# Attention with 64x64 score tiles, paired value products and unpadded q, ahead of two feed-forward nets

## The chip, the core and the metric

The kernel runs on one core of a Trainium2 chip, alone. The core has engines that run side by side, each with its own in-order queue: TensorE (PE; its weight loads are shown apart as PEld), VectorE (DVE), ScalarE (ACT), GpSimd (POOL), and SyncE (SP), which here only issues DMA transfers. [...] The metric is the device time of one execution in microseconds (us); of the kernel before three executions are known.

## What is computed

Banded attention with block summaries, for 2 batches, 8 heads, 768 positions and 64 numbers per head, and then two feed-forward nets on the 1536 x 512 result:

```python
k_sum = k.reshape(B, H, nb, 32, D).max(axis=3)
v_sum = v.reshape(B, H, nb, 32, D).mean(axis=3)
mask_l = np.abs(pos[:, None] - pos[None, :]) < 16
scores_l = where(mask_l, q @ k.T / sqrt(D), -1e9)
scores_s = q @ k_sum.T / sqrt(D) + log(32)
a = softmax(concatenate([scores_l, scores_s], -1))
x = a @ concatenate([v, v_sum], axis=2)      # heads side by side: 1536 x 512
h = x @ w_in;   x = (h - tanh(h)) @ w_out            # first net, 512 -> 2048 -> 512
h = x @ w2_in;  out = (h * tanh(softplus(h))) @ w2_out
```

Everything is float32. The attention's products are plain float32 matmuls; those of the nets are three products of split halves (`xhi`, `xlo`, `ghi`, `glo`, and the two halves of the weights).

## The kernel before

**Attention.** The queries are cut into 12 units u of 128 rows (6 for each batch), and the 8 heads into 4 pairs; head e of a pair (e = 0 or 1) lies on partitions 64e to 64e+63 of q and k. Of a unit's 128 rows, rows 0 to 63 (s = 0) and 64 to 127 (s = 1) each see a window of 96 keys and 24 block summaries, so a score row has 120 columns. In `qk(u, e)` there are 8 matmuls (4 pairs, 2 values of s) of a 128 x 64 piece of q against 128 x 120 of k; the 64 partitions of the other head are zeros in `qz`, so that all 128 partitions can be contracted. The scores of e = 0 go to a PSUM bank of tag `s`, of e = 1 to one of tag `tr`; each tag has two banks. `softmax(u, e)` reduces on DVE and takes the exponent on ACT, `norm(u)` divides (on POOL, four times on DVE), `a_trans(u, e)` turns the weights with 4 full-array transposes into `aT` and has them copied to `asb` (by DVE where the table `ASB_DVE` says so, otherwise by ACT), and `av(u, e)` multiplies them with the values in 8 matmuls of 120 x 64 against 120 x 64, into the half of a bank `x` on partitions 64e to 64e+63. `x_hi` and `x_lo` take the result out. `v_trans` (once for each batch) turns the value summaries through a bank of `tr`.

**What sets the order.** The order is written out by hand. Step j issues, in this order: `x_hi`, `qk` of (u, e) = j, `softmax` of j-1, `norm`, `x_lo`, `a_trans` of j-5, `av` of j-6, and then the DMA loads and reductions of the table `todo`. From step 24 on there are no scores any more, and `more_in` puts first products of the first net (`ffn_in`, 12 matmuls of 512 columns, called FFN-in 0, 1, 2, ... below) between the last steps of attention: FFN-in 0 at step 24, 1 at step 25, 2 at step 29. Behind attention the nets' products follow each other on TensorE. Weights are loaded raw and converted in `conv_tick`, as pieces that go through ACT (`conv_top`, L114), DVE (`conv_or`, L121), ACT or POOL (`conv_hi`, L130, L132) and DVE or POOL (`conv_lo`, L137); FFN-in i needs both of its pieces.

**Loads.** All DMAs are issued by SP in program order. A DMA waits for the one eight before it in that order to have landed (they share a semaphore), and for its tile to be free: q of unit u for the scores of u-3, v of u for the value products of u-3. `load_q(u)` issues two DMAs, of 64 partitions each. `q_zero` writes the zeros once, on DVE and ACT, at the program's start.

Of the kernel before, what the change touches and what calls it, by code (L numbers as in the profile page):

```python
# [9 lines left out]
F32 = mybir.dt.float32  # L10
# [10 lines left out]
BLK, WIN, T = 32, 16, 64  # L21
# [5 lines left out]
def kernel(  # L27
# [17 lines left out]
    nc = tc.nc  # L45
    NU, _, HP, _ = qt_d.shape
# [4 lines left out]
    NB = S // BLK  # L51
    KA = NB + KW
# [25 lines left out]
    def pst(tag):  # L78
        return ps.tile([128, 512], F32, tag=tag, name=tag)
# [99 lines left out]
    def attention(actx):  # L179
# [3 lines left out]
        kq = kq_x.enter_context(tc.tile_pool(name="kq", bufs=1))  # L183

        NK = UPB + 2
        kt = [kq.tile([128, HP, KU + 2 * NB], F32, name=f"kt{n}") for n in range(NK)]
        qz = [kq.tile([128, 2, HP, 128], F32, name=f"qz{n}") for n in range(3)]
        vu = [con.tile([KA, 2, H, D], F32, name=f"vu{n}") for n in range(3)]
        masks = [con.tile([128, KA], F32, name=f"mask{m}") for m in range(3)]
        ident = con.tile([128, 128], F32, name="ident")  # L190
        SUM = ((0, NB), (KW, KA))
        WND = ((NB, KA), (0, KW))

        def q_zero(n):
            for e in range(2):
                other = qz[n][64 * (1 - e):64 * (1 - e) + 64, e]
                if n < 2:
                    nc.vector.memset(other, 0.0)
                else:
                    nc.scalar.copy(other, qz[0][64 * (1 - e):64 * (1 - e) + 64, e])  # L200

        def constants():
            nonlocal tops
            make_identity(nc, ident)
            k_edges(0)
            for m in range(3):
                nc.gpsimd.memset(masks[m], 0.0)
                for s in range(2):
                    rows = masks[m][T * s:T * s + T]
                    nc.gpsimd.memset(rows[:, SUM[s][0]:SUM[s][1]], math.sqrt(D) * math.log(BLK))  # L210
                    reg = rows[:, WND[s][0]:WND[s][1]]

                    conds = [([[1, KW]], -1, -1), ([[-1, KW]], 2 * WIN - 1, 1)]
                    if (m, s) == (0, 0):
                        conds.append(([[1, KW]], -WIN, 0))
                    if (m, s) == (2, 1):
                        conds.append(([[-1, KW]], KW - WIN - 1, 0))
                    for pattern, base, mul in conds:
                        nc.gpsimd.affine_select(
                            out=reg, in_=reg, pattern=pattern, base=base, channel_multiplier=mul,  # L220
                            compare_op=ALU.is_ge, fill=-BIG,
                        )
            k_edges(UPB)
            tops = top_tiles(2)
# [20 lines left out]
                nc.gpsimd.memset(kt[UPB - 1][:, :, r:r + WIN], 0.0)  # L245

        def load_q(u):
            for e in range(2):
                nc.sync.dma_start(out=qz[u % 3][64 * e:64 * e + 64, e], in_=qt_d[u, 64 * e:64 * e + 64])

        def load_v(u):
            for s in range(2):
# [2 lines left out]
        def load_vt(b, g):  # L255
            vtc[b, g] = two.tile([128, HP, 256], F32, tag="vtc", name="vtc", bufs=3)
            nc.sync.dma_start(out=vtc[b, g], in_=vt_d[b, g])
# [48 lines left out]

        sums, neg, aa, asb, xps, sc = {}, {}, {}, {}, {}, {}

        def qk(u, e):
            p = pst(("s", "tr")[e])  # L310
            pv = p[:, 0:HP * KA].rearrange("p (a n) -> p a n", a=HP)
            for hp in range(HP):
                for s in range(2):
                    k0 = s * (NB + T)
                    nc.tensor.matmul(
                        out=pv[T * s:T * s + T, hp, :],
                        lhsT=qz[u % 3][:, e, hp, T * s:T * s + T],
                        rhs=kt[u % NK][:, hp, k0:k0 + KA],
                    )
            sc[u, e] = pv  # L320

        def softmax(u, e):
            w, pv = u % UPB, sc.pop((u, e))
# [37 lines left out]
                nc.scalar.activation(out=t, in_=pv, func=ACTF.Copy)  # L361
            asb[u, e] = t

        def av(u, e):
            if e == 0:
                xps[u] = pst("x").rearrange("p (a n) -> p a n", a=HP)
            for hp in range(HP):
                for s in range(2):
                    nc.tensor.matmul(  # L369
                        out=xps[u][64 * e:64 * e + 64, hp, T * s:T * s + T],  # L370
                        lhsT=vu[u % 3][:, s, 2 * hp + e, :],
                        rhs=asb[u, e][:, hp, T * s:T * s + T],
                    )

        def x_hi(u):
            c, o = divmod(u * 128, CH)
            nc.scalar.activation(out=xhi[c][:, :, o:o + 128], in_=xps[u], func=ACTF.Copy)

        def x_lo(u):
            c, o = divmod(u * 128, CH)  # L380
            nc.vector.tensor_tensor(
                out=xlo[c][:, :, o:o + 128], in0=xps.pop(u),
                in1=xhi[c][:, :, o:o + 128].bitcast(F32), op=ALU.subtract,
            )
# [13 lines left out]
        load_vt(0, 1)  # L398
        load_q(2)
        load_vt(0, 2)  # L400
        for n in range(3):
            q_zero(n)
        constants()
        warm = pst("x")
        for n in range(NWARM):
# [34 lines left out]
        NJ = 2 * NU  # L440
        LT, LA = 5, 6

        def ticks(j, counts):
            for _ in range(counts.get(j, 0)):
                conv_tick(len(pieces) // 2, j in HI_POOL, j in LO_POOL)

        for j in range(NJ + LA + 2):
            if j in (NJ, NJ + 1, NJ + 5):
                more_in(n_in)
            if j == NJ:  # L450
                kq_x.close()
                more_w(4)
            xu, xr = divmod(j - LA - 2, 2)
            if xu >= 0 and not xr:
                x_hi(xu)
            if j < NJ:
                qk(j // 2, j % 2)
            nu, nr = divmod(j - 3, 2)
            nr = nr == 0 and 0 <= nu < NU
            if 1 <= j <= NJ:  # L460
                softmax(*divmod(j - 1, 2))
            ticks(j, AHEAD)
            if nr:
                norm(nu)
            if xu >= 0 and xr:
                x_lo(xu)
            if LT <= j < NJ + LT:
                a_trans(*divmod(j - LT, 2))
            if j in before_av:
                before_av[j]()  # L470
            if LA <= j < NJ + LA:
                av(*divmod(j - LA, 2))
            for f in todo.get(j, []):
                f()
            ticks(j, AFTER)
            if NJ + 2 <= j <= NJ + 3:
                gate_1(steps[j - NJ - 2])
            if j == NJ + 4:
                gate_1s(steps[0])
# [39 lines left out]
    def gate_1s(z):  # L519
        g_hi(z, ts[z])  # L520
        g_lo(z, ts.pop(z))
# [73 lines left out]
    def more_in(n):  # L595
        nonlocal n_in
        while n_in <= min(n, NS - 1):
            ffn_in(*steps[n_in])
            n_in += 1
# [18 lines left out]
    def more_w(n):  # L618
        wb = ctx.enter_context(tc.tile_pool(name=f"wb{len(W)}", bufs=1))
        for i in range(len(W), len(W) + n):  # L620
            W[i] = wb.tile([128, 2, 1024], F32R, name=f"w{i}")

    with tc.manual_schedule():
        with ExitStack() as actx:
            attention(actx)
# [140 lines left out]
```

## Time and profile before

| | us |
|---|---|
| median of 3 runs (lowest, highest) | 611.64 (611.49, 612.99) |
| profiled execution | 611.33 |
| its span, first to last instruction | 609.6 |
| TensorE busy (share of the span) | 594.0 (97%) |
| VectorE busy | 421.1 (69%) |
| ScalarE busy | 330.2 (54%) |
| GpSimd busy | 53.2 (9%) |

Times in the rows are us from the span's start. The profile shows each float32 matmul of the attention as two matmul records; transposes and the nets' products are one record each. Matmuls are pipelined, so a record lasts longer than the step from one record to the next. In a timeline row stand start, length, engine, line, operation, output <- inputs, shape, count, and in brackets the engine's idle time just before it and what ended it. In the chain of waits, which is followed back from the end, stand start, share of time and what it was; there a record counts only for the time it adds. [...]

### The profile page before, as it was taken

The numbers are of one execution on the slowest core, as the hardware profiler recorded it, in microseconds if no ns is written. First come the engines' busy times: TensorE is split into PE (matmuls) and PEld (weight loads), VectorE is DVE, ScalarE is ACT, GpSimd is POOL, SyncE is SP. The second block draws the span as 40 slices with busy tenths as digits, with TensorE's granted clock in tenths as the row PEclk, the third lists the DMA queues.
The fourth block names the chain that finished last, engine by engine and source line by source line (L and its number), as shares of the span: only waits on it lengthen the run. The fifth ranks groups of instructions, "written<-read, shape, count | busy, mean of one in ns | idle before, by whom it ended". The sixth has DMA issues, their size and how long they took to land.

```text
span 609.6 us, 9228 instructions
## 1 busy us (share of the span) xinstructions
PE 594.0 (97%) x3212; PEld 494.0 (81%) x3212; DVE 421.1 (69%) x972; ACT 330.2 (54%) x793; POOL 53.2 (9%) x109
## 2 busy tenths in 40 slices
PE   7698999999999999999999999999999999999997
PEld 6577888888888888888888888888888888888886
DVE  6668967887342222367777579997768777598785
ACT  5678958887242222356776446664454444454442
POOL 5446652000000000000000000000000000000000
PEclk9899999999999999999999999999999999999999
DMA  9999547766121000125662101100010000100001
GB/s 239 232 254 261 162 134 230 230 216 198 45 54 33 1 0 1 34 83 160 198 195 74 52 1 52 53 19 1 1 69 1 1 1 0 70 1 1 1 1 69
DMA packets 32302, 52.20 MB, mean 86 GB/s; under 512 B 3392, under 2 KB 25920, under 8 KB 32256
## 3 DMA queue, kind: packets, MB, share of 16 engines
q1 hardware_dynamic: 32256, 51.62, 29.3%
q8 instruction: 25, 0.41, 0.3%
q14 instruction: 21, 0.17, 0.1%
HBM read 48.07 MB, written 3.15 MB: 84 GB/s over the span
## 4 chain that ended last, share of the span: by engine, by line
PE 90%; DMA 7%; SPq 1%; DVE 1%; POOL 0%; ACT 0%; issue 0%; POOLq 0%
PE s L486 7%; PE aT L486 7%; PE s L487 7%; PE aT L487 7%; PE s L488 7%; PE tr L487 7%; PE x L487 7%; PE aT L488 7%; PE tr L488 7%; PE x L488 7%; PE tr L486 7%; PE x L486 7%; DMA qz<-in_qt_dram 3%; DMA kt<-in_kw_dram 2%; PE x L369 2%; PE aT L355 1%
## 5 line engine op out<-in xcount | busy, mean ns | idle before, releaser
L511 DVE TENSOR_TENSOR glo<-t,ghi 128x512 fp32r<-128x512 f32 x48 | 33.4, 696 | 86.9 <-ACT ghi L506 86.9
L506 ACT ACTIVATE ghi<-t 128x512 fp32r<-128x512 f32 x48 | 30.2, 629 | 97.3 <-PE tr L488 97.3
L486 PE MATMUL s<-xhi,w 128*128 128x512 f32 x192 | 74.9, 390 | 0.0
L486 PE MATMUL aT<-xhi,w 128*128 128x512 f32 x192 | 74.9, 390 | 0.0
L487 PE MATMUL s<-xlo,w 128*128 128x512 f32 x192 | 74.7, 389 | 0.0
L488 PE MATMUL s<-xhi,w 128*128 128x512 f32 x192 | 74.7, 389 | 0.0
L487 PE MATMUL aT<-xlo,w 128*128 128x512 f32 x192 | 74.7, 389 | 0.0
L488 PE MATMUL aT<-xhi,w 128*128 128x512 f32 x192 | 74.7, 389 | 0.0
L114 ACT ACTIVATE top<-raw 128x256 f16<-128x256 bf16 x128 | 61.5, 486 | 12.3 <-ACT w L132 5.3
L121 DVE SCALAR_TENSOR_TENSOR cv<-raw,top 128x256 int32<-128x256 int32 x128 | 55.5, 435 | 11.3 <-ACT top L114 7.7
L132 ACT ACTIVATE w<-cv 128x256 fp32r<-128x256 f32 x120 | 47.6, 402 | 10.7 <-DVE cv L121 9.7
L137 DVE TENSOR_TENSOR w<-cv,w 128x256 fp32r<-128x256 f32 x114 | 48.4, 426 | 0.1
L542 DVE SCALAR_TENSOR_TENSOR t<-n,r 128x512 f32<-128x512 f32 x48 | 33.1, 689 | 17.5 <-ACT r L539 17.3
L335 ACT ACTIVATE aa<-aa,neg 128x120 f32<-128x120 f32 x96 | 36.6, 383 | 15.0 <-DVE neg L330 15.0
L511 DVE TENSOR_TENSOR glo<-n,ghi 128x512 fp32r<-128x512 f32 x48 | 33.1, 690 | 15.3 <-ACT ghi L506 15.3
L506 ACT ACTIVATE ghi<-n 128x512 fp32r<-128x512 f32 x48 | 30.3, 631 | 24.3 <-PE tr L487 16.1
L486 PEld LDWEIGHTS s<-xhi,w 128*128 128x128 f32 x192 | 36.0, 188 | 7.6
L486 PEld LDWEIGHTS aT<-xhi,w 128*128 128x128 f32 x192 | 36.0, 188 | 7.6
L488 PEld LDWEIGHTS s<-xhi,w 128*128 128x128 f32 x192 | 36.1, 188 | 7.5
L488 PEld LDWEIGHTS aT<-xhi,w 128*128 128x128 f32 x192 | 36.1, 188 | 7.5
L487 PEld LDWEIGHTS s<-xlo,w 128*128 128x128 f32 x192 | 36.0, 188 | 7.4
L487 PEld LDWEIGHTS aT<-xlo,w 128*128 128x128 f32 x192 | 36.0, 188 | 7.4
(99 smaller groups left out, 1307.6 us busy)
## 6 DMA issues: line engine op xcount, KB each, us to landing
raw<-in_w_dram SPq DMA_DIRECT2D x128, 255.8 KB, 3.6
vu<-in_vw_dram SPq DMA_DIRECT2D x24, 192.0 KB, 6.0
qz<-in_qt_dram SPq DMA_DIRECT2D x24, 128.0 KB, 6.9
vtc<-in_vt_dram SPq DMA_DIRECT2D x6, 512.0 KB, 6.8
out_dram<-o SPq DMA_DIRECT2D x9, 256.0 KB, 2.1
kt<-in_kw_dram SPq DMA_DIRECT2D x6, 320.0 KB, 6.4
kt<-in_kw_dram SPq DMA_DIRECT2D x6, 256.0 KB, 4.3
out_dram<-t SPq DMA_DIRECT2D x3, 256.0 KB, 2.1
```

Of the source, the lines that this page charges most:

```text
L114: nc.scalar.activation(out=tops[n % len(tops)].bitcast(F16).rearrange("p (n t) -> p n t", t=2)[:, :, 1], in_=raws[n].bitcast(BF16).rearran ...
L121: nc.vector.scalar_tensor_tensor(out=tmps[n], in0=raws.pop(n).bitcast(I32).rearrange("p (n t) -> p n t", t=2)[:, :, 0], scalar=13, in1=top ...
L132: nc.scalar.activation(out=hi, in_=t, func=ACTF.Copy)
L137: (nc.gpsimd if on_pool else nc.vector).tensor_tensor(out=W[i][:, 1, o:o + PW], in0=tmps.pop(n).bitcast(F32), in1=W[i][:, 0, o:o + PW].bit ...
L335: nc.scalar.activation(out=aa[u][:, e, hp, :], in_=aa[u][:, e, hp, :], func=ACTF.Exp, scale=-1.0, bias=neg[u][:, e, hp:hp + 1], accum_out= ...
L369: nc.tensor.matmul(out=xps[u][64 * e:64 * e + 64, hp, T * s:T * s + T], lhsT=vu[u % 3][:, s, 2 * hp + e, :], rhs=asb[u, e][:, hp, T * s:T ...
L486: nc.tensor.matmul(out=out, lhsT=w[0], rhs=x[0], start=first, stop=False)
L487: nc.tensor.matmul(out=out, lhsT=w[0], rhs=x[1], start=False, stop=False)
L488: nc.tensor.matmul(out=out, lhsT=w[1], rhs=x[0], start=False, stop=last)
L506: nc.scalar.activation(out=ghi, in_=t, func=ACTF.Copy)
L511: nc.vector.tensor_tensor(out=glo, in0=t, in1=ghi.bitcast(F32), op=ALU.subtract)
L542: nc.vector.scalar_tensor_tensor(out=ts[z], in0=ns[z], scalar=2.0, in1=rs[z], op0=ALU.add, op1=ALU.mult)
```

## The change

`qk(u)` now issues both heads of a pair in turn, without zeros: a matmul contracts 64 partitions, and four of them (2 values of e, 2 of s) use the four 64 x 64 quarters of the array. `av(u)` issues the two heads in turn, so that consecutive matmuls write different halves of the PSUM partitions. `qk(u)` stands at step 2u, and `av(u)` at step 2u+7, where before the halves stood at 2u, 2u+1 and 2u+6, 2u+7. The zeros go, and q comes in one DMA of 128 partitions. The number of matmuls stays.

```diff
-        def q_zero(n):
-            for e in range(2):
-                other = qz[n][64 * (1 - e):64 * (1 - e) + 64, e]
...
         def load_q(u):
-            for e in range(2):
-                nc.sync.dma_start(out=qz[u % 3][64 * e:64 * e + 64, e], in_=qt_d[u, 64 * e:64 * e + 64])
+            nc.sync.dma_start(out=qt[u % 3], in_=qt_d[u])
...
-        def qk(u, e):
-            p = pst(("s", "tr")[e])
-            pv = p[:, 0:HP * KA].rearrange("p (a n) -> p a n", a=HP)
+        def qk(u):
+            for e in range(2):
+                sc[u, e] = pst(("s", "tr")[e])[:, 0:HP * KA].rearrange("p (a n) -> p a n", a=HP)
             for hp in range(HP):
                 for s in range(2):
-                    k0 = s * (NB + T)
-                    nc.tensor.matmul(
-                        out=pv[T * s:T * s + T, hp, :],
-                        lhsT=qz[u % 3][:, e, hp, T * s:T * s + T],
-                        rhs=kt[u % NK][:, hp, k0:k0 + KA],
-                    )
+                    for e in range(2):
+                        d = slice(64 * e, 64 * e + 64)
+                        k0 = s * (NB + T)
+                        nc.tensor.matmul(
+                            out=sc[u, e][T * s:T * s + T, hp, :],
+                            lhsT=qt[u % 3][d, hp, T * s:T * s + T],
+                            rhs=kt[u % NK][d, hp, k0:k0 + KA],
+                        )
...
-        def av(u, e):
-            if e == 0:
-                xps[u] = pst("x").rearrange("p (a n) -> p a n", a=HP)
+        def av(u):
+            xps[u] = pst("x").rearrange("p (a n) -> p a n", a=HP)
             for hp in range(HP):
                 for s in range(2):
...
+                    for e in range(2):
+                        nc.tensor.matmul(
+                            out=xps[u][64 * e:64 * e + 64, hp, T * s:T * s + T],
...
-            if j < NJ:
-                qk(j // 2, j % 2)
+            if j < NJ and j % 2 == 0:
+                qk(j // 2)
...
-            if LA <= j < NJ + LA:
-                av(*divmod(j - LA, 2))
+            if LA <= j < NJ + LA and (j - LA) % 2:
+                av((j - LA) // 2)
```

TensorE's queue around unit 9 before, from the value products of the end of unit 5 (x) over the scores of unit 9 (s, tr) to the products of unit 6; aT are transposes, and a row counts matmuls of the program:

```order
L369 MATMUL x<-asb,vu_102 64x64 x8
L315 MATMUL s<-kt_90,qz_97 64x120 x8
L355 MATMUL aT<-ident,aa 120x128 x4
L369 MATMUL x<-asb,vu_100 64x64 x8
L315 MATMUL tr<-kt_90,qz_97 64x120 x8
L355 MATMUL aT<-ident,aa 120x128 x4
L369 MATMUL x<-asb,vu_100 64x64 x8
```

The same place with the change:

```order
L285 MATMUL tr<-ident,vsum 24x128 x4
L363 MATMUL x<-asb,vu_102 64x64 x16
L310 MATMUL s<-kt_90,qt_97 64x120
L310 MATMUL tr<-kt_90,qt_97 64x120
...
L349 MATMUL aT<-ident,aa 120x128 x8
L363 MATMUL x<-asb,vu_100 64x64 x16
```

The second half of the scores moved up in front of the transposes, alternating with the first (16 single rows); two sets of transposes now stand together, and both halves of the value products behind them.

SP's queue in step 5 before, from the loads of q for units 4 and 5 to the loads of k for units 9 and 10 (kt_90, kt_91); L303 copies value summaries within SBUF, and DMAHWn is the semaphore that every eighth DMA shares:

```order
L249 DMA qz_98<-in_qt_dram 64x512 [waits DMAHW2_49,PE_49]
L229 DMA kt_89<-in_kw_dram 128x4x160 [waits DVE_49,DMAHW3_49,Activation_49,Pool_49]
L249 DMA qz_99<-in_qt_dram 64x512 [waits DMAHW4_49,PE_49]
L249 DMA qz_99<-in_qt_dram 64x512 [waits DMAHW5_49,PE_49]
L303 DMA vu_101<-vu_100 24x512 [waits DMAHW6_49,Activation_49]
L303 DMA vu_101<-vu_100 24x512 [waits DMAHW7_49,Activation_49]
L303 DMA vu_102<-vu_100 24x512 [waits DMAHW0_49]
L303 DMA vu_102<-vu_100 24x512 [waits DMAHW1_49]
L229 DMA kt_90<-in_kw_dram 128x4x160 [waits DMAHW2_49,DVE_49]
L229 DMA kt_91<-in_kw_dram 128x4x160 [waits DMAHW3_49,DVE_49]
```

And with the change:

```order
L221 DMA kt_96<-in_kw_dram 128x4x160 [waits DMAHW3_49]
L240 DMA qt_98<-in_qt_dram 128x512 [waits DMAHW5_49,PE_49]
L221 DMA kt_89<-in_kw_dram 128x4x160 [waits DVE_49,DMAHW6_49,Activation_49,Pool_49]
L240 DMA qt_99<-in_qt_dram 128x512 [waits DMAHW7_49,PE_49]
L294 DMA vu_101<-vu_100 24x512 [waits DMAHW0_49,Activation_49]
L294 DMA vu_101<-vu_100 24x512 [waits DMAHW1_49,Activation_49]
L294 DMA vu_102<-vu_100 24x512 [waits DMAHW2_49]
L294 DMA vu_102<-vu_100 24x512 [waits DMAHW3_49]
L221 DMA kt_90<-in_kw_dram 128x4x160 [waits DMAHW4_49,DVE_49]
L221 DMA kt_91<-in_kw_dram 128x4x160 [waits DMAHW5_49,DVE_49]
```

Each unit has one DMA less, so "eight before" reaches further back: kt_90 waited for the second half of q of unit 4, and now waits for k of unit 7, which stands before it.

## Rows read from the trace of the kernel before

**Rows 1.** Busy us by stretch (instructions in brackets), PEclk, DMA share, GB/s

```profile
core 0: us, PE busy (x) PEld busy (x) DVE busy (x) ACT busy (x) POOL busy (x), PEclk, DMA share, GB/s
...
10.35:22.42 12.07, 8.70 (x105) 7.28 (x105) 9.59 (x57) 8.43 (x41) 7.14 (x17) 0.86 1.06 262
...
39.20:58.43 19.23, 16.79 (x239) 14.35 (x237) 18.67 (x91) 15.46 (x66) 12.57 (x22) 1.00 1.04 253
58.43:73.46 15.03, 15.03 (x216) 12.99 (x217) 13.36 (x64) 13.23 (x58) 7.66 (x13) 1.00 0.59 167
73.46:91.42 17.96, 17.96 (x155) 14.79 (x153) 11.79 (x29) 11.80 (x33) 10.35 (x14) 1.00 0.50 144
91.42:605.80 514.38, 514.37 (x2270) 425.59 (x2268) 351.72 (x672) 265.48 (x540) 4.42 (x7) 1.00 0.20 62
```

**Rows 2.** TensorE's waits from 58.6 us on: total, times, longest

```profile
PE s L315 <- DMA qz<-in_qt_dram: 0.5, 1, 0.5
```

**Rows 3.** The chain that ended last: start, us, what

```profile
50.90 7.48 DMA qz<-in_qt_dram
...
68.51 0.88 PE s L315 x15
69.39 0.58 PE aT L355 x4
69.97 1.02 PE x L369 x15
```

**Rows 4.** The DMA engines at 28 us, and SP's issues then

```profile
28.00:30.00 2.00, 1.33 (x26) 1.33 (x28) 1.97 (x11) 2.00 (x11) 1.04 (x2) 1.00 0.50 118
...
28.42 1.51 SPq L229 DMA_DIRECT2D kt<-in_kw_dram  x2
```

**Rows 5.** DVE's timeline: start, us, operation, idle before and what ended it

```profile
4.04 1.51 DVE L264 TENSOR_REDUCE ksum<-kt 128x16 f32<-128x512 f32 x2 [0.73 <-DMA kt<-in_kw_dram]
...
60.09 0.69 DVE L359 COPY asb<-aT 120x512 f32<-120x512 f32 x1 [1.43 <-PE aT L355]
...
70.36 0.68 DVE L359 COPY asb<-aT 120x512 f32<-120x512 f32 x1
...
78.25 1.04 DVE L347 TENSOR_TENSOR aa<-aa,rd 128x480 f32<-128x480 f32 x1
...
81.45 0.69 DVE L359 COPY asb<-aT 120x512 f32<-120x512 f32 x1 [1.57 <-PE aT L355]
```

**Rows 6.** TensorE's timeline, same columns

```profile
17.07 1.22 PE L315 MATMUL s<-kt,qz 128*64 128x120 f32 x15 [2.53 <-DMA qz<-in_qt_dram]
...
68.18 0.32 PE L315 MATMUL s<-kt,qz 128*64 128x120 f32 x1
...
68.35 0.22 PE L369 MATMUL x<-asb,vu 120*64 120x64 f32 x1
...
73.46 0.50 PE L486 MATMUL s<-xhi,w 128*128 128x512 f32 x1
...
85.74 0.65 PE L355 MATMUL aT<-ident,aa 128*120 128x128 f32 x4
...
91.42 0.50 PE L486 MATMUL aT<-xhi,w 128*128 128x512 f32 x1
...
94.27 0.39 PE L486 MATMUL s<-xhi,w 128*128 128x512 f32 x1
```

**Rows 7.** ACT's and POOL's timelines, same columns

```profile
57.39 1.18 ACT L296 ACTIVATE vu<-tr 24x512 f32<-24x512 f32 x2
...
86.49 0.60 ACT L361 ACTIVATE asb<-aT 120x512 f32<-120x512 f32 x1
...
74.75 0.75 POOL L137 TENSOR_TENSOR w<-cv,w 128x256 fp32r<-128x256 f32 x1
...
79.51 0.98 POOL L347 TENSOR_TENSOR aa<-aa,rd 128x480 f32<-128x480 f32 x1
...
91.58 2.56 POOL L137 TENSOR_TENSOR w<-cv,w 128x256 fp32r<-128x256 f32 x3 [1.42 <-ACT w L132]
```

More of the change, by code (lines that the diff above doesn't have):

```diff
@@ L186, in attention @@
         kt = [kq.tile([128, HP, KU + 2 * NB], F32, name=f"kt{n}") for n in range(NK)]
-        qz = [kq.tile([128, 2, HP, 128], F32, name=f"qz{n}") for n in range(3)]
+        qt = [kq.tile([128, HP, 128], F32, name=f"qt{n}") for n in range(3)]
         vu = [con.tile([KA, 2, H, D], F32, name=f"vu{n}") for n in range(3)]
@@ L192, in attention @@
         WND = ((NB, KA), (0, KW))
-        def q_zero(n):
-            for e in range(2):
-                other = qz[n][64 * (1 - e):64 * (1 - e) + 64, e]
[L197 to L200, printed above, removed]
         def constants():
@@ L307, in attention @@
         sums, neg, aa, asb, xps, sc = {}, {}, {}, {}, {}, {}
-        def qk(u, e):
-            p = pst(("s", "tr")[e])
-            pv = p[:, 0:HP * KA].rearrange("p (a n) -> p a n", a=HP)
+        def qk(u):
+            for e in range(2):
+                sc[u, e] = pst(("s", "tr")[e])[:, 0:HP * KA].rearrange("p (a n) -> p a n", a=HP)
             for hp in range(HP):
                 for s in range(2):
-                    k0 = s * (NB + T)
-                    nc.tensor.matmul(
-                        out=pv[T * s:T * s + T, hp, :],
-                        lhsT=qz[u % 3][:, e, hp, T * s:T * s + T],
-                        rhs=kt[u % NK][:, hp, k0:k0 + KA],
-                    )
-            sc[u, e] = pv
+                    for e in range(2):
[6 more added lines that the diff above has]
+                        )
         def softmax(u, e):
@@ L362, in a_trans @@
             asb[u, e] = t
-        def av(u, e):
-            if e == 0:
-                xps[u] = pst("x").rearrange("p (a n) -> p a n", a=HP)
+        def av(u):
+            xps[u] = pst("x").rearrange("p (a n) -> p a n", a=HP)
             for hp in range(HP):
                 for s in range(2):
[L369 to L373, printed above, removed]
+                    for e in range(2):
+                        nc.tensor.matmul(
+                            out=xps[u][64 * e:64 * e + 64, hp, T * s:T * s + T],
+                            lhsT=vu[u % 3][:, s, 2 * hp + e, :],
+                            rhs=asb[u, e][:, hp, T * s:T * s + T],
+                        )
         def x_hi(u):
@@ L400, in attention @@
         load_vt(0, 2)
-        for n in range(3):
-            q_zero(n)
         constants()
```

## The prediction

> **What bounds the kernel now.** I read the table by stretch first, then TensorE's waits, then the chain, then the timelines of the engines that the chain names. The table [rows 1] shows four stages. Up to 58.43 us the DMA engines are full (share 1.04 in 39.20 to 58.43), and so, in that stretch, is DVE (18.67 of 19.23 us). From 58.43 on TensorE has no idle time until its last matmul at 605.80: its only wait there is 0.5 us for q of unit 9, at 58.43 itself [rows 2]. That q is the last link of the DMA stage: 7.48 us in the queue from 50.90 on [rows 3]. So what the change saves before 58.43 is worth only what it makes that q (and DVE's work beside it) come earlier, and what it saves behind 91.42 is nothing, since there it touches nothing: 514.37 us of net products stay. The time is set by when the nets' products run without a break. The gain must come from 58.43 to 91.42, 33.0 us in which attention's last units share TensorE with FFN-in 0, 1 and 2.
>
> **What one product costs.** In the chain, 15 or 16 score records take 0.88 us, four transposes 0.58 and 15 value records 1.02 [rows 3]. The scores of one half already use two column tiles (s = 0 and 1) at once, the value products of one half only one. That column tiles do run side by side is in the trace: the first score record starts at 68.18, while value records on other columns go on until one that starts at 68.35 [rows 6]. So a value pair of 32 records should take what 16 take now, 1.05 us for 2.1. For the scores the two heads now lie on different rows of the array, and no row of the trace shows two row tiles at once: 32 records take between 0.88 us (four at once) and 1.76 (two at once). I take 0.88, since the same engine overlaps column tiles without loss, and keep 1.76 as a rival. [...]
>
> Per unit TensorE saves 0.9 + 1.05, or about 2 us. In 58.43 to 91.42 stand the scores of units 9, 10, 11 and the value products of 6 to 11: 3 x 0.9 + 6 x 1.05 = 9 us less work in 33. That would be the gain if TensorE alone set the time. It will not, because DVE is nearly as full in the first half: 13.36 of 15.03 us, and 1.43 of the rest is one wait, before 60.09 [rows 1, 5].
>
> **58.43 to 73.46.** DVE stands idle for 1.43 us until 60.09, for transposes queued behind the scores of unit 9 [rows 5]. Those scores took 1.04 us for one half; both halves now take 0.9. Their second bank is the one that `v_trans` used, which ACT empties at 58.57 (57.39 + 1.18) [rows 7], 0.14 behind the start at 58.43. So DVE's work starts at 60.1 as before, and it runs through the same list at the same pace. TensorE, now early, waits for it: the value products of unit 8 need DVE's copy of 70.36 [rows 5], which ends at 71.04. Before, they were done at 73.46; now 71.04 + 1.05 = 72.1. FFN-in 0, whose weights are long ready, starts 1.4 us earlier. A wait for DVE takes the place of most of TensorE's saving (5.9 us saved to here, 1.4 gained); queued behind the waiting value products is FFN-in 0 and nothing that DVE needs soon.
>
> **73.46 to 94.27.** An FFN-in takes 2.85 us (91.42 to 94.27) [rows 6]. From 72.1: FFN-in 0 and transposes to 75.5. FFN-in 1 needs the weight piece that POOL ends at 75.50 (74.75 + 0.75) [rows 7], so it just runs: to 78.4, transposes to 79.0, value pair of unit 9 to 80.05, transposes to 80.6. The next transposes need POOL's product that ends at 80.49 [rows 7]: to 81.2. The value pair of unit 10 needs two copies by DVE. The first stood at 81.45 and had waited 1.57 us for TensorE; DVE is done with its normalisation at 79.29 (78.25 + 1.04) [rows 5] and has one 0.7 us subtraction in between, so the copies end by 81.5. The pair runs to 82.6, and the last transposes to 83.2, which before started at 85.74 and ended at 86.4 [rows 6]: 3.2 us earlier. FFN-in 2 to 86.05, last value pair to 87.1, where it was 91.42: 4.3 us earlier.
>
> But FFN-in 4 had no slack. Its weight pieces left POOL at 94.14 (91.58 + 2.56) [rows 7], and it started at 94.27 [rows 6]. These pieces go through ACT behind its last copy, which stood at 86.49 [rows 7] and waited for those last transposes. They move by 3.2 us, to 90.9, while TensorE would be there at 87.1 + 2.85 = 89.95. It waits about 1 us, and from there everything is 3.3 us earlier. **This term: -3.3 us**; bounds -2.4 (a part of the conversions that does not move with ACT) and -4.3 (all of it does).
>
> **The DMA stage.** At 28 to 30 us the DMA share falls to 0.50 [rows 4], the one gap of the stage: 1.0 us lost. SP was held in the copies of value summaries and issued the next k at 28.42. With one DMA less per unit the "eight before" of that k is an earlier transfer, so it goes out sooner. If the gap closes, every later landing, and DVE's full stretch that begins at 39.20, moves up. Bounds: 0, if SP is held elsewhere, and -1.0. **I take -0.5.** I see no loss here: the bytes and their order are the same.
>
> **At nothing.** The removed zeros stand on DVE and ACT in the first 3.3 us; DVE's next work still waits for k at 4.04 [rows 5], so that wait covers them. Twelve issues on SP fewer: SP is ahead of the DMA engines. The value products of the first half, now one step later, have no reader before the second half is done.
>
> Changing modes is a price. At 68.18 the scores slip in among value records since both use 64-column tiles of all rows [rows 6]; with 64 x 64 tiles they may not, which costs that 0.17 us, and the first record in a new shape takes 0.50 for 0.39 (73.46 against 94.27) [rows 6]. [...] By the rows the price is at most 0.3 us per unit, and TensorE waits for DVE where it falls; at the value pairs behind 73.46 the modes are those of before. [...]
>
> **Sum.** 0.5 + 3.3 = 3.8 us. The profiled execution took 611.33 (span 609.6 and 1.7 around it), 0.3 less than the median of 611.64. It would take 607.5; against the median that is 607.8.
>
> **Rivals.** (1) The row halves run one after the other: the scores of unit 9 take 1.76, DVE starts 0.7 later, and with it all that follows: 608.5. For it: no row of the trace shows row tiles.
>
> (2) TensorE's clock falls once near 58 us. [...] With the change TensorE has about half the work in the DMA stage: 16.79 less some four units at 2 us, in 19.23 us. If a low stretch meets the scores of unit 9, these and the transposes take 2.9 for 1.5 us, and DVE starts 1.4 later: 609.2. Against it: in 39.20 to 58.43 TensorE idled 2.4 us in all and PEclk stayed 1.00 [rows 1].
>
> (3) Nothing runs side by side as meant (tiles collide, or issue is too slow): the work is as before, DVE waits 0.7 us more at 60.09, FFN-in follows as it did, and the DMA term stays: 611.1 to 612, no change.
>
> [...]
>
> **How the numbers follow.** Forecast 0.52 (606 to 609, by the bounds of its two terms), rival 1 0.11, rival 2 0.16 (608.7 to 610.5), rival 3 0.12, rival 4 0.09. Time: 607.8. The range goes from 605.8, both terms at their best and half a us more, to 610.8, which takes in rival 2 and a little of rival 3 and leaves out about 0.2. A difference under 0.3% (1.8 us: 609.8 and 613.5) can hardly be told from none. Faster: 0.52 + 0.11 + half of rival 2 = 0.71; same: the other half and most of rival 3 = 0.19; slower 0.10.
>
> **What would show it.** Right: a value pair in about 1.05 us and 32 score records in 0.9; DVE's copy at 60.1 or up to 1 us earlier, and its list until 76 unchanged; TensorE idle before the value products of unit 8, for DVE's copy, and before FFN-in 4, for POOL; FFN-in 0 near 72 and FFN-in 4 near 90.5. The prediction is wrong if q of unit 9 lands later than 58.4, if PEclk drops below 1.00 behind 55 us, if score records of the two heads never start closer than those of one, or if TensorE waits again behind 95 us.

## The result, and the profile after

The changed kernel took 602.73 us (median of 4, 602.28 to 604.61) where the kernel before took 612.32 beside it (4 runs, 611.49 to 613.78): a ratio of 0.9846, 95% interval 0.982 to 0.9872. The forecast was 607.8 with a range of 605.8 to 610.8, so the direction was right and the gain of 9.6 us was two and a half times the forecast 3.8; the time lies below the range. The profiled execution took 603.07 us, with a span of 601.3 where before had 609.6. Each kernel below was run beside the kernel before, but not all of them on the same chip, so across kernels the ratio compares better than the time. Executions more than 1.5% above the quickest of their kernel are left out of the ratios, not of the medians.

First the table by stretch of the changed kernel, which answers [rows 1] (busy us by engine, then PEclk, the granted TensorE clock with 1.00 as full speed, DMA share, GB/s). Its stretches are cut at its own events: k of unit 11 landed, scores of unit 9 (all but two records that started at 53.05), FFN-in 0, FFN-in 3, last matmul.

```profile
core 0: us, PE busy (x) PEld busy (x) DVE busy (x) ACT busy (x) POOL busy (x), PEclk, DMA share, GB/s
34.58:54.65 20.07, 13.72 (x253) 11.17 (x253) 18.33 (x92) 16.03 (x67) 12.73 (x22) 0.91 0.96 274
54.65:68.29 13.64, 11.82 (x215) 9.95 (x215) 11.94 (x59) 11.60 (x51) 6.96 (x12) 0.87 0.51 149
68.29:83.09 14.80, 14.64 (x155) 11.91 (x152) 11.48 (x31) 12.69 (x38) 11.04 (x15) 1.00 0.55 163
83.09:597.50 514.41, 514.38 (x2272) 425.74 (x2268) 352.86 (x675) 265.70 (x541) 4.42 (x8) 1.00 0.20 63
```

The last stretch is what it was (514.41 us for 514.37), so all of the gain lies ahead of FFN-in 3, as the prediction said. The timelines then show in which part. DVE's, which answers [rows 5] (the copy behind the scores of unit 9 stood at 60.09, that of unit 8's weights at 70.36):

```profile
34.58 0.69 DVE L255 TENSOR_REDUCE ksum<-kt 128x16 f32<-128x512 f32 x1 [1.31 <-DMA kt<-in_kw_dram]
...
56.31 0.69 DVE L353 COPY asb<-aT 120x512 f32<-120x512 f32 x1 [1.63 <-PE aT L349]
...
66.47 0.68 DVE L353 COPY asb<-aT 120x512 f32<-120x512 f32 x1
```

And TensorE's, which answers [rows 6] (four scores of unit 9, value products of units 7 and 8, FFN-in 0, the last value pair, FFN-in 3 and 4):

```profile
54.65 0.31 PE L310 MATMUL tr<-kt,qt 64*64 64x120 f32 x1 [1.18 <-ACT vu L287]
54.65 0.31 PE L310 MATMUL s<-kt,qt 64*64 64x120 f32 x1
54.66 0.31 PE L310 MATMUL tr<-kt,qt 64*64 64x120 f32 x1
54.67 0.31 PE L310 MATMUL s<-kt,qt 64*64 64x120 f32 x1
...
62.11 1.15 PE L363 MATMUL x<-asb,vu 120*64 120x64 f32 x30 [1.65 <-DVE asb L353]
...
66.80 1.56 PE L363 MATMUL x<-asb,vu 120*64 120x64 f32 x32
68.29 0.50 PE L478 MATMUL s<-xhi,w 128*128 128x512 f32 x1
...
82.01 1.15 PE L363 MATMUL x<-asb,vu 120*64 120x64 f32 x32
83.09 0.50 PE L478 MATMUL aT<-xhi,w 128*128 128x512 f32 x1
...
85.95 0.39 PE L478 MATMUL s<-xhi,w 128*128 128x512 f32 x1
```

Below, **the mark** is DVE's copy at 60.09 before and 56.31 after: it is the same instruction of the program in all kernels, the first that follows the scores of unit 9. The span then falls into four parts:

| part | before | after | difference | forecast |
|---|---|---|---|---|
| start to the mark | 60.09 | 56.31 | -3.8 | -0.5 |
| the mark to FFN-in 0 | 13.37 | 11.98 | -1.4 | -1.4 |
| FFN-in 0 to FFN-in 3 | 17.96 | 14.80 | -3.2 | -3.0 |
| FFN-in 3 to the end | 518.2 | 518.2 | 0 | +1.0 |

Two terms miss: the DMA stage by 3.3 us, and the wait at FFN-in 4 by 1.0.

Where the DMA stage gained is seen in the list of DMA issues (number, KB each, median us from issue to landing). Of the kernel before:

```profile
vu<-in_vw_dram SPq DMA_DIRECT2D x24, 192.0 KB, 6.0
qz<-in_qt_dram SPq DMA_DIRECT2D x24, 128.0 KB, 6.9
```

Of the changed kernel:

```profile
vu<-in_vw_dram SPq DMA_DIRECT2D x24, 192.0 KB, 4.9
qt<-in_qt_dram SPq DMA_DIRECT2D x12, 256.0 KB, 4.9
```

The loads of v were not touched, and they land in 4.9 us instead of 6.0. A q of 256 KB lands sooner than a half of 128 KB did. The bytes flow faster while the DMA share says "full" in both: from 40 to 50 us the kernel before moved 259 GB/s at a share of 1.04 (its row stands below), and the changed kernel

```profile
40.00:50.00 10.00, 7.38 (x138) 6.39 (x138) 8.67 (x45) 9.38 (x42) 7.97 (x17) 0.83 1.06 321
```

### The profile page after: what moved, and what is told of

It reads as the page before. It is cut to its first block, busy times and chain, and to the rows that moved or that the text cites. A ratio compares the mean times of both kernels' runs of the same rounds, so it can differ in the third digit from the quotient of the medians.

```text
span 601.3 us, 9203 instructions
## 1 busy us (share of the span) xinstructions
PE 578.8 (96%) x3212; PEld 479.0 (80%) x3212; DVE 417.8 (69%) x968; ACT 328.5 (55%) x791; POOL 53.4 (9%) x109
## 4 chain that ended last, share of the span: by engine, by line
PE 88%; DMA 4%; DVE 3%; ACT 2%; SPq 1%; issue 1%; POOL 0%; ACTq 0%
PE aT L478 7%; PE aT L479 7%; PE tr L479 7%; PE x L479 7%; PE aT L480 7%; PE tr L480 7%; PE x L480 7%; PE x L478 7%; PE tr L478 7%; PE s L479 7%; PE s L478 7%; PE s L480 7%; DMA kt<-in_kw_dram 3%; ACT aa L329 1%; DMA vtc<-in_vt_dram 1%; PE x L363 1%
```

## The experiments

**The two halves of the change apart.** My theory after the result was A: the loads of q, in one DMA of 128 partitions, shorten the DMA stage. The rival B: the shorter TensorE work releases tiles sooner, and the loads follow. Two kernels undo one half each, and two more split the loads and the value products.

Undo the loads alone:

```diff
-            nc.sync.dma_start(out=qt[u % 3], in_=qt_d[u])
+            for e in range(2):
+                nc.sync.dma_start(out=qt[u % 3][64 * e:64 * e + 64], in_=qt_d[u, 64 * e:64 * e + 64])
```

> The changed kernel with q loaded as before, in two DMAs of 64 partitions for each unit; all else stays. The changed kernel took 602.7 us (0.9846 of the kernel before), 5.8 us less than my sum for it had from the DMA stage and the tail at their middle; by its trace DVE's copy behind the scores of unit 9 stood 3.8 us earlier, where I had 0.5. Theory A (the loads of q: one DMA of 128 partitions makes the DMA stage shorter): those 3.8 us go, 606.5 us, and that copy stands near 60. Rival B (the order on TensorE: half as long scores and products release tiles sooner, and the loads follow): 602.7, the copy near 56.3.

Measured: 609.67 us, 0.9976 of before (0.995 to 1.0002), with the mark at 61.45. Nearly all of the gain is gone: theory A, and more than the 3.8 us it had asked for. The tail kept its part (11.98 us from the mark to FFN-in 0, 14.82 from there to FFN-in 3).

Keep the loads, undo the order on TensorE (the scores still contract 64 partitions, without zeros):

```diff
-        def qk(u):
+        def qk(u, e):
...
-            if j < NJ and j % 2 == 0:
-                qk(j // 2)
+            if j < NJ:
+                qk(j // 2, j % 2)
...
-            if LA <= j < NJ + LA and (j - LA) % 2:
-                av((j - LA) // 2)
+            if LA <= j < NJ + LA:
+                av(*divmod(j - LA, 2))
```

> The order of the kernel before on TensorE (one half of the scores and of the value products in each step), with q without zeros in one DMA; so at most two tiles can run side by side. Theory A (loads of q): it keeps the 3.8 us of the DMA stage and nothing of the tail: 608.5 us, 0.994 of the kernel before. Rival B (order): as the kernel before, 612.

Measured: 612.41 us (608.11 to 618.30, ten runs), 1.0007 (0.9969 to 1.0045), with the mark at 59.68. Theory A fails here as it stood: taken together, the runs show no gain from the quick loads alone. Why is in the table by stretch. The kernel before:

```profile
30.00:40.00 10.00, 9.37 (x136) 7.99 (x133) 5.28 (x31) 7.18 (x31) 2.82 (x3) 1.00 1.03 262
40.00:50.00 10.00, 9.28 (x136) 7.99 (x134) 9.85 (x50) 7.47 (x33) 7.36 (x13) 1.00 1.04 259
```

The old order with the quick loads:

```profile
30.00:40.00 10.00, 10.00 (x135) 8.69 (x133) 7.72 (x44) 8.01 (x34) 2.20 (x3) 0.92 0.70 209
40.00:50.00 10.00, 10.00 (x140) 8.41 (x138) 8.43 (x45) 8.52 (x35) 7.45 (x14) 1.00 0.82 259
```

The DMA share falls to 0.70 and 0.82: the loads are no longer the limit. But TensorE (first number) is busy for 10.00 of 10.00 us. Its timeline in that run repeats without a gap:

```profile
41.83 1.04 PE L306 MATMUL s<-kt,qt 64*64 64x120 f32 x16
42.80 0.65 PE L345 MATMUL aT<-ident,aa 128*120 128x128 f32 x4
43.38 1.15 PE L359 MATMUL x<-asb,vu 120*64 120x64 f32 x16
44.46 1.04 PE L306 MATMUL tr<-kt,qt 64*64 64x120 f32 x16
```

A step of half a unit takes 44.46 - 41.83 = 2.63 us, 5.25 for a unit. In the kernel before, the scores of units 5 to 9 followed each other by 5.7 to 6.3 us, at a DMA share of 1.02 to 1.06. So TensorE's limit lay close below that of the loads, and the change lowers both.

By these paces this kernel should gain some 0.4 to 1.1 us for each unit. Against that stands the clock: from the first scores of unit 3 to those of unit 4 TensorE was never idle and its granted clock was 0.50, and half a unit took 4.73 us where it later took 2.63, which is 4.2 us for the two halves. Their rows, the old order with the quick loads:

```profile
21.58:26.31 4.73, 4.73 (x36) 3.97 (x37) 2.23 (x13) 1.82 (x8) 0.81 (x1) 0.50 1.04 299
26.31:31.04 4.73, 4.73 (x37) 3.97 (x36) 2.74 (x17) 2.30 (x11) 1.93 (x2) 0.50 0.60 159
```

The kernel before had a clock of 1.00 in that part (22.42 to 29.43 us). The three quickest of the ten runs, at 608.1 to 608.4 us, came out at theory A's 608.5; their mean clock was 0.988 to 0.990, that of the others 0.974 to 0.986. Lowering one limit alone thus gained almost nothing as measured (0.9976 and 1.0007), and both together give 0.9846; how much the quick loads alone would gain at full clock, no run shows.

**What of the loads.** q in two DMAs of 128 partitions:

```diff
-            nc.sync.dma_start(out=qt[u % 3], in_=qt_d[u])
+            for e in range(2):
+                nc.sync.dma_start(out=qt[u % 3][:, 2 * e:2 * e + 2], in_=qt_d[u][:, 2 * e:2 * e + 2])
```

> The changed kernel with q in two DMAs of 128 partitions, each with two of the four pairs of heads: as many DMAs as before the change, but no half of the partitions left out. Theory A1 (transfers of 64 partitions are slow and hold the others up): 602.7, as the changed kernel. Theory A2 (the number of DMAs: one more for each unit, so that eight before in the order reaches less far back and SP is held longer): 606.5. Rival B (TensorE's order): 602.7.

Measured: 604.93 us, 0.99 (0.9866 to 0.9934), the mark at 58.58. It lies clear of the halves (0.995 to 1.0002): with as many DMAs, most of the gain is there. Then two DMAs of 64 partitions, but of every second one:

```diff
-            nc.sync.dma_start(out=qt[u % 3], in_=qt_d[u])
+            for e in range(2):
+                nc.sync.dma_start(out=qt[u % 3][e:128:2], in_=qt_d[u, e:128:2])
```

> The changed kernel with q in two DMAs of 64 partitions, as in the run with halves (0.9976), but of every second partition, where that one took the lower 64 and then the upper 64; packets of 2048 bytes and 24 DMAs in both. [...] Theory N (64 partitions as such, fewer packets in each DMA, are slow): 0.9976 and near 142 ns.

Measured: 603.5 us, 0.988 (0.9847 to 0.9912), the mark at 56.35. Same number of DMAs, same bytes and rows as the halves, and the loss is gone. So it is not the 64 partitions, it is which 64. The packets of 2048 bytes took 124 ns on average ahead of 58 us, with halves 142; those of 4096 bytes, which belong to loads that neither kernel touches, 191 and 231. With halves TensorE's clock was lower too (0.50 from 20 to 30 us, here 0.73), and what that adds to the loss is not separated by these two. DVE's row at the mark, with halves and then with every second partition:

```profile
61.45 0.69 DVE L354 COPY asb<-aT 120x512 f32<-120x512 f32 x1 [1.79 <-PE aT L350]
```

```profile
56.35 0.69 DVE L354 COPY asb<-aT 120x512 f32<-120x512 f32 x1 [2.16 <-PE aT L350]
```

**The price of the way by itself.** A kernel without attention and nets only loaded q, in four ways:

```diff
+        for rep in range(3):
+            for load in (whole, halves, every_second, pairs):
+                for u in range(8):
+                    load(u)
```

> No attention and no nets: only q of 8 units is loaded, 12 times over, each time in one of four ways: whole (128 partitions in one DMA), lower and upper 64 partitions, every second partition, two pairs of heads each; then one column of each tile is read, and the next 8 units follow. The output is zeros. It measures the price of the way by itself. If the half of the partitions is what is slow, the 2 MB in halves take longer and their packets of 2048 bytes are slower than those of every second partition, by about the 15 to 20% that the stage showed (142 against 120 ns). If the ways are alike here, halves cost only where other loads run beside them.

It could not decide: SP mostly needed 0.54 to 0.59 us to issue each DMA of 64 partitions, so only some 205 GB/s were asked for and the DMA engines were not full (with halves 207 GB/s at a share of 0.6 to 0.7 from 45.8 to 48.7 us; with every second partition 211 at 0.71 from 17.00 to 25.40 us and 203 at 0.70 from 51.00 to 59.90). The next kernel put 512 KB of v beside each q:

```diff
+                for u in range(6):
+                    nc.sync.dma_start(out=v[u], in_=vt_d[u // NG, u % NG])
+                    load(u)
```

> Loads alone again (no attention, no nets, zeros as output), now with 512 KB of v beside the q of each of 6 units, in three ways for q: whole, lower and upper 64 partitions, every second partition; each 6 units (4.7 MB) and then the next, three times over. SP can put out over 400 GB/s so, and the DMA engines are the limit. If halves are slow beside other loads: 4.7 MB in halves take at least a tenth longer than with every second partition (16 us for 14.5, by 142 and 120 ns a packet on a third of the bytes and what lies beside them). If not: alike, and the price in the attention stage comes from something else in it.

Its table by stretch (length, DVE and POOL busy, PEclk, DMA share, GB/s), in the order whole, halves, every second partition, and that three times:

```profile
6.00:13.00 7.00, 0.65 (x6) 0.00 (x0) 1.00 1.04 409
18.00:29.00 11.00, 1.07 (x9) 0.00 (x0) 1.00 1.05 322
31.00:41.00 10.00, 1.28 (x10) 0.00 (x0) 1.00 1.04 402
43.00:52.00 9.00, 1.28 (x10) 0.00 (x0) 1.00 1.03 400
56.00:70.00 14.00, 1.28 (x10) 0.00 (x0) 1.00 1.04 283
72.00:82.00 10.00, 1.28 (x10) 0.00 (x0) 1.00 1.03 398
84.00:93.00 9.00, 1.28 (x10) 0.00 (x0) 1.00 1.04 403
97.00:112.00 15.00, 1.28 (x10) 0.00 (x0) 1.00 1.04 260
114.00:122.00 8.00, 1.03 (x8) 0.00 (x0) 1.00 1.04 394
```

This settles it. With q in halves everything moves at 260 to 322 GB/s, with q whole or in every second partition at 394 to 409, though only a third of the bytes is q. And the DMA share reads 1.03 to 1.05 in all nine rows, at 260 GB/s as at 409: slow packets fill it as well as quick ones. The transfers beside such a load are slowed with it: the packets of v, 4096 bytes each, took 161 to 170 ns on average beside whole q and every second partition, and 201, 231 and 254 beside halves. Why a load into the lower or the upper 64 partitions is slow, and one into every second partition is not, was not shown.

**The number of DMAs.** Another DMA of 2 KB for each unit:

```diff
+        spare = [kq.tile([1, HP, 128], F32, name=f"spare{n}") for n in range(3)]
...
             nc.sync.dma_start(out=qt[u % 3], in_=qt_d[u])
+            nc.sync.dma_start(out=spare[u % 3], in_=qt_d[u, 0:1])
```

> The changed kernel with a second DMA behind each q, of one row of q (2 KB) into a spare tile that nothing reads: 24 DMAs for q as before the change, and practically no more bytes. Theory C (the number of DMAs holds SP, since each waits for the one eight before): 0.990, as with q in two DMAs of 128 partitions, 2 to 3 us over the changed kernel. Rival (those 2 to 3 us are the smaller packets, 1024 bytes, of that run): 0.9846.

Measured: 603.97 us, 0.9885 (0.9859 to 0.9912). And q of two units in one DMA:

```diff
-            nc.sync.dma_start(out=qt[u % 3], in_=qt_d[u])
+            if u % 2 == 0:
+                nc.sync.dma_start(
+                    out=qt[u // 2 % 3], in_=qt_d[u:u + 2].rearrange("u p a n -> p u a n")
+                )
...
-                            lhsT=qt[u % 3][d, hp, T * s:T * s + T],
+                            lhsT=qt[u // 2 % 3][d, u % 2, hp, T * s:T * s + T],
```

> The changed kernel with q of two units in one DMA of 128 partitions (6 DMAs instead of 12, 512 KB each, issued where the first unit's q was). If the number of DMAs counts (theory C): 1 us less, 0.983. If the time is now set elsewhere in the stage (DVE, ACT): 0.9846. If larger transfers delay k and v behind them: slower, 0.987.

Measured: 605.5 us, 0.9902 (0.9866 to 0.9938). More DMAs and fewer both lie 1 to 3 us above the changed kernel, within what the intervals leave open. Theory C (their number) finds no support: by it, fewer should have been quicker. It is not excluded either, since a DMA of two units may hold up the loads behind it.

**The order on TensorE, part by part.** Value products in turn instead of in pairs, at the same step:

```diff
-            for hp in range(HP):
-                for s in range(2):
-                    for e in range(2):
+            for e in range(2):
+                for hp in range(HP):
+                    for s in range(2):
                         nc.tensor.matmul(
                             out=xps[u][64 * e:64 * e + 64, hp, T * s:T * s + T],
```

> The changed kernel with the two halves of the value products one after the other, at the same step; scores and loads as changed. What is lost is 1.05 us on TensorE for each of the value pairs of units 9, 10 and 11, where no other engine covers it, and less for those before: 3 to 4.5 us, 606 to 607. The DMA stage keeps its 3.8 us under theory A. If instead the scores gave the tail, 603.

Measured: 604.68 us, 0.9891 (0.9851 to 0.993), the mark at 54.58. From FFN-in 0 to 3 it took 83.00 - 66.56 = 16.44 us, 1.64 more than the changed kernel, and from the mark to FFN-in 0 the same 11.98, so the tail lost 1.64 and not 3 to 4.5. The scores of the two heads in turn, in the same manner:

```diff
-            for hp in range(HP):
-                for s in range(2):
-                    for e in range(2):
+            for e in range(2):
+                for hp in range(HP):
+                    for s in range(2):
                         d = slice(64 * e, 64 * e + 64)
```

> The changed kernel with the scores of the two heads one after the other (16 records of one half, then 16 of the other), at the same step; value products and loads as changed. So at most two tiles run side by side in the scores. Theory T (row halves run side by side when they alternate, and only then): a unit's scores take 1.6 us instead of 0.8 to 0.9, and of the 26.8 us from DVE's copy behind the scores of unit 9 to FFN-in 3 under 1 us is lost, since DVE's list covers the scores of units 10 and 11: 0.9855 to 0.987 of the kernel before. Rival (the engine takes them side by side in either order, or never): no change, 0.9846.

Measured: 603.17 us, 0.988 (0.9841 to 0.9919); from the mark (57.50) to FFN-in 3 (84.29) 26.79 us, in the changed kernel 26.78. A unit's scores took 1.25 us from the first start to the last, not 1.6 (in the changed kernel 0.8), since the two halves overlap in the middle even so. Nothing of that shows in the tail: DVE's list covers it.

Scores as changed, value products in the old order:

```diff
-        def av(u):
+        def av(u, e):
...
-            if LA <= j < NJ + LA and (j - LA) % 2:
-                av((j - LA) // 2)
+            if LA <= j < NJ + LA:
+                av(*divmod(j - LA, 2))
```

> The scores as changed (both heads at one step, in turn, four tiles), q in one DMA, but the value products of each half at its own step as before. Theory P: TensorE needs some 0.8 us less for each unit, so the DMA stage comes back too; in the tail the value pairs' 1.6 us are missing: 0.989 of the kernel before, and 28.4 us from DVE's copy behind the scores of unit 9 to FFN-in 3. If the gain needs the value pairs, 0.997.

Measured: 605.66 us, 0.9881 (0.9851 to 0.9911), the mark at 55.92. Its FFN-in 0 and FFN-in 3:

```profile
67.90 0.50 PE L478 MATMUL s<-xhi,w 128*128 128x512 f32 x1
...
85.85 0.50 PE L478 MATMUL aT<-xhi,w 128*128 128x512 f32 x1
```

That stretch takes 17.95 us, as before the change (17.96), where I expected less. The other way round, value products as changed and scores in the old order:

```diff
-        def qk(u):
+        def qk(u, e):
...
-            if j < NJ and j % 2 == 0:
-                qk(j // 2)
+            if j < NJ:
+                qk(j // 2, j % 2)
```

> The value products as changed (both halves at one step, in turn), q in one DMA without zeros, but the scores of each half at its own step as before. Theory P (with the quick loads, TensorE's own pace of 5.25 us for each unit is what held the run in the old order; it needs both, less work on TensorE and quicker loads): TensorE needs some 0.9 us less for each unit, so most of the 3.8 us of the DMA stage comes back, and in the tail the 1.6 us that the value pairs are worth: 0.991 of the kernel before. If the old order was held by something else than TensorE's pace: 0.997.

Measured: 607.06 us, 0.9865 (0.9802 to 0.9928), with times from 600.55 to 613.12. The profile is of the longest of these, with the mark at 61.84 and a granted clock of 0.50 from 62 to 70 us. The same kernel once more:

> The kernel with the value products alone as changed (scores of each half at its own step, q in one DMA), once more. Theory P (TensorE's pace held the old order): DVE's copy behind the scores of unit 9 between 55 and 58, as in the changed kernel, where the old order with the same loads had 59.7; about 0.99 of the kernel before. Otherwise that copy near 59.7 and 0.997.

Measured: 602.02 us (601.50 to 615.41, four runs), 0.983 (0.9784 to 0.9876), the mark at 55.10 and

```profile
67.07 0.50 PE L474 MATMUL s<-xhi,w 128*128 128x512 f32 x1
...
81.87 0.50 PE L474 MATMUL aT<-xhi,w 128*128 128x512 f32 x1
```

So it has 11.97 and 14.80 us in the two stretches of the tail, the same as the whole change. In these two profiles either part alone brings the mark to 55 or 56 (theory P: less work on TensorE, whichever, is what the quick loads needed). TensorE's pace shows it: a unit took 4.2 us with the value products alone (from the scores of unit 5 to those of unit 6, below) and 4.3 with the scores alone (33.80 to 38.09), where the old order took 5.25.

```profile
32.96 1.04 PE L306 MATMUL s<-kt,qt 64*64 64x120 f32 x16
...
37.14 1.04 PE L306 MATMUL s<-kt,qt 64*64 64x120 f32 x16
```

The third part of the table, FFN-in 0 to 3, belongs to the value products alone: 1.64 us to their running in pairs, the other 1.5 to both halves standing at one step. The four score tiles add nothing that these runs can show.

**One link loosened.** In the changed kernel the scores of unit 9 wait 1.18 us for ACT's copy of the value summaries, and DVE 1.63 in turn (the rows at 54.65 and 56.31 above). A kernel turns the summaries one step later:

```diff
-        before_av[17] = L(v_trans, 1)
-        at(17, L(v_fill, 1), L(v_fill, 2))
+        before_av[18] = L(v_trans, 1)
+        at(18, L(v_fill, 1), L(v_fill, 2))
```

> The changed kernel with the second batch's value summaries turned (v_trans, and the copies that follow from it) at step 18 instead of 17, behind the scores of unit 9 and the transposes of unit 6, not ahead of them. In the changed kernel half the scores of unit 9 waited 1.2 us for ACT's copy out of their bank, and DVE 1.63 us in turn until its copy at 56.31. If that is the last link between the DMA stage and the tail: 1.2 to 1.6 us less than the changed kernel on this chip, about 0.998 of it. If DVE's copy is then held by something that ends as late (the reduction of the value summaries, the softmax): the same as the changed kernel.

> The changed kernel itself, on the chip of these runs, so that the others stand against it: 0.9846 of the kernel before, 26.8 us from DVE's copy behind the scores of unit 9 to FFN-in 3, and that copy near 56.3.

Measured beside each other: 602.74 us (601.78 to 604.64) against 603.6 (603.17 to 604.39) for the changed kernel, which is 0.9842 of before (0.9811 to 0.9873) and so as first measured, with its mark at 57.58 and 26.83 us from there to FFN-in 3. The later turn had its mark at 54.71. The difference in time can't be told from none. Both once more, with six runs each:

> The changed kernel with the value summaries turned behind the scores of unit 9, once more, in five rounds: 1.2 us less than the changed kernel beside it if that wait is the last link, no less if something else ends as late.

> The changed kernel once more, in five rounds, for the run beside it: 0.9844 of the kernel before.

Measured: 601.87 us (601.24 to 602.69) against 604.57 (602.78 to 604.88): 2.7 us by the medians, with no overlap, where the first pair had overlapped. DVE's mark in the two, the changed kernel last:

```profile
53.50 0.69 DVE L353 COPY asb<-aT 120x512 f32<-120x512 f32 x1 [0.96 <-PE aT L349]
```

```profile
56.14 0.69 DVE L353 COPY asb<-aT 120x512 f32<-120x512 f32 x1 [1.63 <-PE aT L349]
```

So turning the summaries later brings the mark 2.6 us ahead (2.9 in the first pair), more than the wait of 1.18 itself. Half of that is given back: from the mark to FFN-in 3 that run takes 28.09 us (81.59 - 53.50) instead of 26.76, with a clock of 0.93 and 0.94 in the two parts of it. Its scores of unit 9 now wait 1.77 us for their q, so the loads are the next link again. Against before the two stand at 0.9832 (0.98 to 0.9864) and 0.987 (0.9834 to 0.9907). The kernel with the value products alone reached the same times in some runs, but its eight runs spread from 600.55 to 615.41 us.

## Why the prediction was right or wrong

**The DMA stage, -0.5 for -3.8: the step that failed.** The prediction said "I see no loss here: the bytes and their order are the same", and took as the only gain the gap at 28 us [rows 4]. It read the share of 1.04 in [rows 1] as DMA engines at their limit, so that only a gap could give time. The same row said 253 GB/s; the kernel that only loads q and v shows 400 at the same share. The price of a load was taken from its bytes, and where it lands was not asked. The bounds (0 and -1.0) came from the gap and so left out the transfers themselves. The rest of the first part held for the changed kernel: the 3.8 us ahead of the mark are all there at the end.

**Full twice.** The prediction named DMA and DVE as full up to 58.43. It had TensorE's 16.79 of 19.23 us in view, and used it for the clock alone. In the old order with quick loads TensorE had no idle time from 21.58 us on. The shorter TensorE work thus had a second worth that no term priced: without it the gain of the loads did not appear (1.0007). The clock had a part in it, and no term had it in the DMA stage: it stood at 0.50 there for both halves of a unit.

**The mark to FFN-in 0, -1.4 for -1.4: right, and for the reason given.** DVE runs through the same list at the same pace and sets the end. The table of that stretch alone, of the changed kernel in its first and in its last profile, shows 11.91 us of DVE in 11.98 both times:

```profile
56.31:68.29 11.98, 10.16 (x181) 8.45 (x179) 11.91 (x57) 9.94 (x45) 6.37 (x9) 0.86 0.45 130
```

```profile
56.14:68.12 11.98, 8.55 (x180) 7.07 (x179) 11.91 (x57) 9.94 (x45) 6.37 (x9) 1.00 0.50 146
```

TensorE's wait that I had placed before the value products of unit 8 lies before those of unit 7 (1.65 us at 62.11).

**FFN-in 0 to 3, -3.2 for -3.0: right.** The chain of weights, transposes, copies and pairs of the prediction fits to 0.2 us. A value pair took 83.09 - 82.01 = 1.08 us for the 1.05 forecast.

**The wait at FFN-in 4, +1.0 for 0: wrong.** The prediction let FFN-in 4 wait for the pieces that POOL ends at 94.14 [rows 7]. In the changed kernel POOL's row is

```profile
84.50 2.56 POOL L137 TENSOR_TENSOR w<-cv,w 128x256 fp32r<-128x256 f32 x3 [1.41 <-ACT w L132]
```

and ends at 87.06, while FFN-in 4 began at 85.95 without a wait. The start of a group of 12 matmuls is not when its last piece of weights is read: by the program the last of these three pieces is the second half of FFN-in 4's, and its result is first read by the ninth matmul, which began at 87.76. That the two stood 0.13 us apart before was taken as cause; TensorE had no wait there before either, since 91.42 and the 2.85 us of an FFN-in make 94.27. The bound of -4.3 for the tail was nearly the right value (-4.6 measured).

**The rivals.** Rival 1 (row halves one after the other) falls: four score records start within 0.02 us at 54.65, and a unit's 32 in 0.8 us. In turn, at 1.25 us for a unit, they cost the tail nothing either (26.79 us from the mark to FFN-in 3). Rival 3 (nothing side by side) falls with it. Rival 2 came true in part of its condition and not in its price (its 2.9 us for 1.5 takes half the clock, and the low stretches of these traces read 0.50, as 18.00 to 20.00 us of the kernel before do): TensorE's clock fell, but at the scores of unit 11 and not of unit 9 (PEclk 0.50 in this row of the table by stretch of the changed kernel),

```profile
63.30:66.60 3.30, 3.30 (x40) 2.90 (x40) 3.30 (x12) 2.62 (x10) 3.17 (x4) 0.50 0.46 110
```

and the stretch from the mark to FFN-in 0 still took 11.98 us, as it did with the clock at 1.00 (the two rows above), because DVE sets its length. The prediction had also named a clock below 1.00 behind 55 us as a sign of being wrong; by these rows it was none. Rival 4, the slower outcome at 0.09, did not come: the low clock lasted some 3.4 us in the changed kernel's tail and had ended before FFN-in 0 (PEclk 1.00 from 66.80 to 73.00 us).

**Mode changes** were priced at no more than 0.3 us for a unit, off the path. Before, the undisturbed scores stood 2.37 and 2.59 us apart in turn; in the old order with 64 x 64 tiles 2.63. That is 0.14 for a half, 0.3 for a unit: the size was right, but in that kernel TensorE is the limit and it is on the path. That it is the change of mode, and not something else about the smaller tiles, was not tested apart.

**What stays open.** How the 3.8 us ahead of the mark divide between the loads and TensorE's work can't be said, since neither alone brings them. Which of the DMA engines' packets waited for which can't be seen in the trace. The differences of 1 to 3 us between the changed kernel and the variants with one more or fewer DMAs were not resolved. The loads of v, which fill 96 partitions, may be held in the same way as q was; that was not tried.

## What to carry to other kernels

A DMA share near 1 does not mean that the DMA engines move all they can (here 1.03 to 1.05 went with 260 to 409 GB/s): read GB/s beside it, and ask of each load which partitions it fills. When one limit is lifted, look up what the next engine's busy time is in the same stretch, and at which clock; two limits close to each other hide each other, and two edits that each measure as almost nothing can be worth 1.5% together, as here (0.9976 and 1.0007, and 0.9846). A term for a wait needs the instruction that reads the late piece, not the group that it stands in.

## What the runs showed of the hardware

- Loads into the lower and the upper 64 partitions, with other loads beside them, moved 260 to 322 GB/s in all; whole loads or loads into every second partition 394 to 409. With nothing beside them, at the some 205 GB/s that SP asked for, halves showed no loss: 207 GB/s, where every second partition moved 203 to 211.
- Four tiles of 64 x 64 do run at once in plain float32: records on the four quarters start some 7 ns apart, and 32 of them in the 0.8 us that 16 took on two tiles.
- Even in turn, the two halves of the scores overlap where one ends and the other begins: 1.25 us for 32 records.
- With loads alone, SP mostly took 0.54 to 0.59 us to issue a DMA of 64 partitions, halves or every second one, and 0.38 to 0.43 for one of 128 partitions with half the columns.
